# The second parts of the first 16 weight tiles move from GpSimd to VectorE

## The chip, the cores and the metric

The kernel runs on one core of a Trainium2 chip. The metric is the device time of one execution in microseconds (us); the median of several executions is compared. PE is TensorE, DVE is VectorE, ACT is ScalarE, POOL is GpSimd, and SP is the queue that issues every load and store of this kernel.

## The reference

Retention (attention without softmax, with a decaying mask) over 8 batches and 8 heads gives 4608 rows of 512; a feed-forward layer with a rational activation follows, all in float32. The weights arrive as float64.

```python
scores = scale * np.matmul(q, k.transpose(0, 1, 3, 2))       # 8, 8, 576, 576
ret = scores * Dmat[None, :, :, :]                           # gamma ** (i - j), lower triangle
x = np.matmul(ret, v)                                        # then rows of B * S, H * D = 4608, 512
h = x @ w_in                                                 # w_in 512, 2048
h2 = h * h; h3 = h2 * h
P = a[0] + a[1] * h + a[2] * h2 + a[3] * h3
Q = 1.0 + np.abs(b[0]) * np.abs(h) + np.abs(b[1]) * h2
out = (P / (Q + 1e-06)) @ w_out                              # w_out 2048, 512
```

## The kernel before

**Two parts of each operand.** TensorE multiplies in a rounded 32-bit format. To keep precision, x, g (the activation) and the weights are held as a rounded part and the rest, and every product is three matmuls: first times first, first times second, second times first.

**Weights.** There are 32 weight tiles of 128 x 512: `in 0` to `in 15` (w_in, used by `gemm1`) and `out 0` to `out 15` (w_out, used by `gemm2`). Each is loaded as float64 words (`bits`) and made into float32 on the chip by `split_weight`, in four steps with a `yield` between: ACT takes the absolute value of the upper words into `c`; DVE shifts `c` (TENSOR_SCALAR, called **the shift** here); two scalar_tensor_tensor operations on DVE put in the lower bits (`low`) and the sign (`high`, called **the last combine**); then ACT writes the first part `w[:, 0]` (**the copy**) and GpSimd writes the second part `w[:, 1] = c - w[:, 0]` (**the subtraction**). `c` has four buffers, freed by the subtraction. The order in which the tiles are needed is `order`: in 0, in 1, in 2, in 3, out 0, in 4, out 1, in 5, out 2, in 6, out 3, in 7, out 4, out 5, out 6, out 7 are its first 16, and its last 16 follow.

**Units and steps.** There are 36 units of 128 rows of the retention. For each, GpSimd scales q (`scale_q`), ACT scales v, TensorE makes `scores`, DVE multiplies them by the mask (`decay`, tile `s`), TensorE makes `outputs`, ACT and DVE split the result into `xhi` and `xlo`, and DVE and GpSimd update the state `S_sb` (`add`, `fade`). The first units run before the feed-forward part begins (`before`), the others inside its steps. A step (b, f) makes 128 columns of h for 512 rows: `gemm1` on TensorE, then `ffn_p` (ACT and DVE), `ffn_p2` (DVE, called **p2**; it frees the buffer of h, of which there are two), `ffn_v`, and one step later `ffn_r` (ACT: Ln, Exp) and `ffn_q` on DVE, whose first operation is called **q1** here. `ffn_hi` and `ffn_lo` split g; in the first 24 steps `ffn_lo` runs on GpSimd. `gemm2` adds g times w_out three or four steps later.

**What sets the order.** Each of the engines PE, ACT, DVE and POOL runs its instructions in the order in which the Python code calls them (class `InOrder`); only SP's order is left to the scheduler. Within a step the order is that of a list of names: `BEFORE` for the first units, `FIRST` for steps 0 to 23, and others after that. In `FIRST` the last combine (`split2`) is followed, for DVE, by what `split3` gives it (nothing so far), then `add`, `keep_lo` and p2:

```python
FIRST = (
    "split1 gemm1 outputs ffn_p split2 ffn_hi keep_hi ffn_lo gemm2 ffn_r scale_q split3 add fade keep_lo start ffn_p2"
    " scale_v scores decay split0 ffn_q ffn_v"
).split()
```

`STARTS` says how many weight tiles a step takes up. Of the first 16 tiles, in 0 to in 3 are finished before step 0; out 0 and in 4 in step 0; then step 1: out 1; step 2: in 5; step 3: out 2 and in 6; step 4: out 3; step 5: in 7 and out 4; steps 6, 7 and 8: out 5, out 6 and out 7.

Of the kernel before, what the change touches and what calls it, by code (L numbers as in the profile page):

```python
# [12 lines left out]
F32 = mybir.dt.float32  # L13
# [5 lines left out]
ALU = mybir.AluOpType  # L19
# [10 lines left out]
NF = DFF // P  # L30
# [36 lines left out]
def retention_ffn(ctx: ExitStack, tc: tile.TileContext, qkv, w_in, w_out, ab, masks, gq, gv, out):  # L67
# [22 lines left out]
    pe, act, dve, pool = (InOrder(tc, e) for e in (nc.tensor, nc.scalar, nc.vector, nc.gpsimd))  # L90
# [48 lines left out]
    def split_weight(k):  # L139


        nm = f"{k[0]}_{k[1]}"
        words = bits[k].bitcast(I32).rearrange("p (c w) -> p c w", w=2)
        low, high = words[:, :, 0], words[:, :, 1]
        c = cnv.tile([P, DM], I32, tag="c", name=f"c{nm}")
        cf = c.bitcast(F32)


        act.activation(cf, high.bitcast(F32), AF.Abs, scale=math.ldexp(1.0, -112))
        yield  # L150
        dve.tensor_scalar(c, c, 3, 1, ALU.logical_shift_left, ALU.bitwise_or)
        yield
        dve.scalar_tensor_tensor(c, low, 29, c, ALU.logical_shift_right, ALU.bitwise_or)
        yield
        dve.scalar_tensor_tensor(c, high, -0x80000000, c, ALU.bitwise_and, ALU.bitwise_or)
        yield
        w = wts.tile([P, 2, DM], F32R, tag=f"w{nm}", name=f"w{nm}")
        del bits[k]
        act.activation(w[:, 0, :], cf, AF.Copy)
        pool.tensor_tensor(w[:, 1, :], cf, w[:, 0, :].bitcast(F32), ALU.subtract)  # L160
        parts[k] = w


# [228 lines left out]
    order = [(w, f) for _, w, f in sorted(need)]  # L392
# [7 lines left out]
    def split_start(n):  # L400
        for k in [k for _, k in zip(range(n), splits)]:
            going.append([split_weight(k), 0])
            next(going[-1][0])
# [119 lines left out]
```

## Time and profile before

| what | value |
|---|---|
| time, median of 3 runs (lowest to highest) | 989.28 us (988.65 to 990.79) |
| the profiled execution's own time | 987.99 us |
| its span, first to last instruction | 986.2 us |
| busy share PE, DVE, ACT, POOL | 94%, 84%, 72%, 15% |
| mean granted TensorE clock | 0.985 |

The shares are means over stages with different limits: TensorE is busy nearly all the time only from about 250 us on, and all 32 weight tiles are made before that. A timeline row gives start, duration and engine, and in brackets how long the engine had been idle and what ended that.

### The profile page before, as it was taken

The page shows a single profiled execution, that of the slowest core. Times are in us where ns is not written, and L with a number is a line of the kernel's source. Part 1 is how long each engine was busy: PE and PEld are TensorE (multiplying, and loading weights), DVE is VectorE, ACT ScalarE, POOL GpSimd, SP SyncE. Part 2 cuts the span into 40 slices and gives each one's busy share as a digit, 9 for nine tenths or more (in the row PEclk, how much of TensorE's full clock was granted, in tenths as well). Part 3 has the DMA queues.
Part 4 walks back from the last instruction along what each step waited for, and adds up shares of the span by engine and source line. Part 5 has one row for each costly group of instructions (what it writes and reads, how often), then busy time and mean ns, then how long its engine had stood idle before and what let it go on. Part 6 is the DMA issues. An engine that isn't in the chain of part 4 may idle for free.

```text
span 986.2 us, 14758 instructions
## 1 busy us (share of the span) xinstructions
PE 929.7 (94%) x5658; PEld 752.2 (76%) x5658; DVE 829.3 (84%) x1189; ACT 708.0 (72%) x1274; POOL 146.1 (15%) x128
## 2 busy tenths in 40 slices
PE   7769878779999999999999999999999999999998
PEld 6557666567787888788888888888888888888886
DVE  3899989998789888888888887888788888888895
ACT  5577777778676777777777777777777777777775
POOL 3445333442100000000000000100000000000000
PEclk8799999999999999999999999999999999999999
DMA  9945000003212111210021112110211121001001
GB/s 346 407 160 213 1 0 1 1 0 109 91 59 86 44 44 41 71 56 22 32 81 44 44 44 86 44 65 22 86 44 44 43 86 44 1 1 44 1 1 43
DMA packets 20550, 65.31 MB, mean 66 GB/s; under 512 B 2304, under 2 KB 2432, under 8 KB 20480
## 3 DMA queue, kind: packets, MB, share of 16 engines
q1 hardware_dynamic: 20480, 64.37, 17.9%
q8 instruction: 44, 0.72, 0.3%
q14 instruction: 26, 0.21, 0.1%
HBM read 54.93 MB, written 9.44 MB: 65 GB/s over the span
## 4 chain that ended last, share of the span: by engine, by line
PE 71%; DVE 19%; ACT 5%; issue 3%; DMA 1%; SPq 0%; ACTq 0%; DVEq 0%
PE acc L63 32%; PE h L63 31%; PE ps L63 8%; DVE c L63 8%; DVE p L63 7%; DVE v L63 2%; ACT c L63 1%; ACT u L63 1%; DMA kv<-in_qkv 1%; ACT kv L63 1%; ACT v L63 1%; DVE s L63 1%; ACT o L63 1%; DMA qk<-in_qkv 0%; DVE xlo L63 0%
## 5 line engine op out<-in xcount | busy, mean ns | idle before, releaser
L63 PE MATMUL acc<-w,g 128*128 128x512 f32 x1632 | 402.3, 396 | 5.1 <-ACT o L63 4.0
L63 PE MATMUL h<-xhi,w 128*128 128x512 f32 x1152 | 381.9, 393 | 18.5 <-DVE p L63 17.3
L63 PEld LDWEIGHTS acc<-w,g 128*128 128x128 f32 x1632 | 303.3, 189 | 76.4 <-ACT o L63 4.8
L63 PEld LDWEIGHTS h<-xhi,w 128*128 128x128 f32 x1152 | 216.8, 188 | 70.0 <-DVE p L63 22.7
L63 PE MATMUL h<-xlo,w 128*128 128x512 f32 x576 | 225.1, 391 | 0.2 <-DVE xlo L63 0.2
L63 ACT ACTIVATE p<-h,ab_sb 128x512 f32<-128x512 f32 x144 | 111.4, 773 | 138.7 <-PE h L63 131.5
L63 DVE TENSOR_TENSOR p<-p,h 128x512 f32<-128x512 f32 x144 | 98.9, 687 | 44.3 <-ACT u L63 44.0
L63 DVE SCALAR_TENSOR_TENSOR p<-p,ab_sb,u 128x512 f32<-128x512 f32 x144 | 108.9, 756 | 27.0 <-ACT u L63 26.3
L63 ACT ACTIVATE u<-h 128x512 f32<-128x512 f32 x144 | 85.6, 595 | 60.0 <-DVE v L63 58.5
L63 PEld LDWEIGHTS h<-xlo,w 128*128 128x128 f32 x576 | 108.4, 188 | 22.5 <-DVE xlo L63 0.5
L63 DVE TENSOR_TENSOR v<-v,u 128x512 f32<-128x512 f32 x144 | 99.5, 691 | 27.8 <-ACT v L63 27.7
L63 ACT ACTIVATE v<-u,absb 128x512 f32<-128x512 f32 x144 | 116.3, 808 | 1.4 <-DVE p L63 1.1
L63 DVE SCALAR_TENSOR_TENSOR p<-p,ab_sb,h 128x512 f32<-128x512 f32 x144 | 107.1, 744 | 3.1
L63 ACT ACTIVATE u<-u,lnb 128x512 f32<-128x512 f32 x144 | 104.5, 725 | 4.7
L63 POOL TENSOR_TENSOR S_sb<-S_sb,gv_sb 128x256 f32<-128x256 f32 x32 | 20.4, 638 | 575.8 <-DVE S_sb L63 572.6
L63 DVE SCALAR_TENSOR_TENSOR p<-v,p 128x512 f32<-128x512 f32 x144 | 100.6, 699 | 5.0
L63 ACT ACTIVATE u<-v,lnb 128x512 f32<-128x512 f32 x144 | 103.3, 718 | 0.2 <-DVE v L63 0.2
L63 DVE SCALAR_TENSOR_TENSOR v<-v,u 128x512 f32<-128x512 f32 x144 | 99.4, 691 | 0.0
L63 DVE TENSOR_TENSOR g<-p,g 128x512 fp32r<-128x512 f32 x112 | 90.2, 805 | 1.4 <-ACT g L63 1.4
L63 ACT ACTIVATE g<-p 128x512 fp32r<-128x512 f32 x136 | 85.7, 630 | 6.9 <-DVE p L63 3.3
L63 ACT ACTIVATE kv<-kv,gv_sb 128x64 f32<-128x64 f32 x288 | 72.6, 341 | 10.0 <-DMA gv_sb<-in_gv 6.3
L63 DVE SCALAR_TENSOR_TENSOR c<-bits,c 128x512 int32<-128x512 int32 x64 | 57.8, 914 | 0.1
(35 smaller groups left out, 623.7 us busy)
## 6 DMA issues: line engine op xcount, KB each, us to landing
qk<-in_qkv SPq DMA_DIRECT2D x36, 512.0 KB, 4.8
kv<-in_qkv SPq DMA_DIRECT2D x36, 512.0 KB, 3.9
bits<-in_w_in SPq DMA_DIRECT2D x16, 512.0 KB, 10.2
bits<-in_w_out SPq DMA_DIRECT2D x16, 512.0 KB, 10.2
out<-o SPq DMA_DIRECT2D x16, 512.0 KB, 3.2
out<-o SPq DMA_DIRECT2D x4, 256.0 KB, 2.3
gq_sb<-in_gq SPq DMA_DIRECT2D x1, 256.0 KB, 2.7
mask_sb<-in_masks SPq DMA_DIRECT2D x1, 128.0 KB, 6.3
```

What stands on the lines that cost most here:

```text
L63: return lambda *a, **k: self.tc.keep_in_program_order(method(*a, **k))
```

## The change

For the first 16 tiles of `order` the subtraction is issued on DVE; for the last 16 it stays on GpSimd.

```diff
         act.activation(w[:, 0, :], cf, AF.Copy)
-        pool.tensor_tensor(w[:, 1, :], cf, w[:, 0, :].bitcast(F32), ALU.subtract)
+
+        engine = dve if order.index(k) < NF else pool
+        engine.tensor_tensor(w[:, 1, :], cf, w[:, 0, :].bitcast(F32), ALU.subtract)
         parts[k] = w
```

(`NF` is 16.) On GpSimd 16 subtractions disappear and nothing else changes place. On DVE 16 appear. The first piece is DVE in step 3, where two tiles (out 2 and in 6, written w_2 and w_6 with c_2 and c_6) are finished; p_3 is that step's `ffn_p2` and s the decay of a unit.

```order
 L63 SCALAR_TENSOR_TENSOR c_2_600<-bits_2_484,c_2_600 128x512
 L63 SCALAR_TENSOR_TENSOR c_6_602<-bits_6_486,c_6_602 128x512
+L63 TENSOR_TENSOR w_2_666<-c_2_600,w_2_666 128x512
+L63 TENSOR_TENSOR w_6_669<-c_6_602,w_6_669 128x512
 L63 SCALAR_TENSOR_TENSOR p_3_641<-p_3_641,ab_sb,h_3_626 128x512
 L63 TENSOR_TENSOR s_684<-ps_675,mask_sb 128x1024
```

The two subtractions stand directly behind the two last combines and ahead of p2 and the decay. The second piece is DVE in step 6 (out 5) and at the start of step 7's work, in the changed kernel: c_5 is the last combine, c_6 the shift of the next tile, p_5 with u_5 is q1.

```order
L63 SCALAR_TENSOR_TENSOR c_5_840<-bits_5_622,c_5_840 128x512
L63 TENSOR_TENSOR w_5_931<-c_5_840,w_5_931 128x512
L63 TENSOR_TENSOR S_sb<-S_sb,ps_843 128x256
L63 TENSOR_TENSOR xlo_458<-ps_843,xhi_457 128x4x128
L63 SCALAR_TENSOR_TENSOR p_6_908<-p_6_908,ab_sb,h_6_865 128x512
L63 TENSOR_SCALAR c_6_937<-c_6_937 128x512
L63 SCALAR_TENSOR_TENSOR p_5_811<-p_5_811,ab_sb,u_5_809 128x512
```

Only the row of w_5 is new there; the six others stood in this order before. The third piece is SP's queue, where the loads of one later unit (qk_734 and kv_736, unit 8) and of weight tiles stand.

```order
-L102 DMA qk_734<-in_qkv 128x1024
-L104 DMA kv_736<-in_qkv 128x1024
 L137 DMA bits_11_1096<-in_w_out 128x512
 L137 DMA bits_15_1098<-in_w_in 128x512
 L137 DMA bits_12_1150<-in_w_out 128x512
+L104 DMA kv_736<-in_qkv 128x1024
+L102 DMA qk_734<-in_qkv 128x1024
```

The unit's two loads move behind three weight loads; the rest of SP's order is as it was.

## Rows read from the trace of the kernel before

**Rows 1.** Windows: length, busy PE, PEld, DVE, ACT, POOL, then clock, DMA, GB/s.
```profile
300.00:350.00 50.00, 49.43 (x316) 40.14 (x315) 43.35 (x64) 35.78 (x66) 3.75 (x4) 1.00 0.18 64
```
**Rows 2.** Chain that ended last, 50 to 112 us, by line.
```profile
by line: DVE c L63 43.3%; DVE p L63 29.1%; DVE v L63 8.6%; issue 7.1%; DVE s L63 5.5%; DVE xlo L63 2.9%; ACT c L63 2.1%; DVE S_sb L63 1.6%; ACT w L63 0.1%
```
**Rows 3.** Tiles c and g: count, duration in ns (min/median/max), first and last start.
```profile
L63 DVE TENSOR_SCALAR c<-c x32: 412/1070/1520, 18.5 to 220.9; 128x512 int32<-128x512 int32 x32
L63 DVE TENSOR_TENSOR g<-p,g x112: 678/684/1334, 240.8 to 977.9; 128x512 fp32r<-128x512 f32 x112
```
**Rows 4.** Timeline, step 7 (out 6): start, duration, engine, instruction.
```profile
101.36 1.19 DVE L63 SCALAR_TENSOR_TENSOR c<-bits,c 128x512 int32<-128x512 int32 x1
102.48 0.73 DVE L63 SCALAR_TENSOR_TENSOR p<-p,ab_sb,h 128x512 f32<-128x512 f32 x1
103.80 1.07 DVE L63 TENSOR_SCALAR c<-c 128x512 int32<-128x512 int32 x1 [0.59 <-ACT c L63]
104.79 0.74 DVE L63 SCALAR_TENSOR_TENSOR p<-p,ab_sb,u 128x512 f32<-128x512 f32 x1
102.59 0.63 ACT L63 ACTIVATE w<-c 128x512 fp32r<-128x512 f32 x1 [0.82 <-DVE c L63]
103.29 1.30 POOL L63 TENSOR_TENSOR w<-c,w 128x512 fp32r<-128x512 f32 x1 [1.29 <-ACT w L63]
```
**Rows 5.** Timeline, step 1 (out 1): the copy and q1.
```profile
51.88 0.63 ACT L63 ACTIVATE w<-c 128x512 fp32r<-128x512 f32 x1
54.07 0.74 DVE L63 SCALAR_TENSOR_TENSOR p<-p,ab_sb,u 128x512 f32<-128x512 f32 x1
```
**Rows 6.** Timeline, step 2 (in 5): GpSimd's scaling of q, the copy, two shifts.
```profile
58.46 1.75 POOL L63 TENSOR_TENSOR qk<-qk,gq_sb 128x512 f32<-128x512 f32 x1
59.08 0.64 ACT L63 ACTIVATE w<-c 128x512 fp32r<-128x512 f32 x1 [0.42 <-DVE c L63]
60.56 1.94 DVE L63 TENSOR_SCALAR c<-c 128x512 int32<-128x512 int32 x2
```
**Rows 7.** Timeline, step 3 (out 2, in 6): both copies, the decay, q1.
```profile
68.60 1.23 ACT L63 ACTIVATE w<-c 128x512 fp32r<-128x512 f32 x2 [2.00 <-DVE c L63]
69.75 1.21 DVE L63 TENSOR_TENSOR s<-ps,mask_sb 128x1024 f32<-128x1024 f32 x1
72.02 0.74 DVE L63 SCALAR_TENSOR_TENSOR p<-p,ab_sb,u 128x512 f32<-128x512 f32 x1
```
**Rows 8.** Timeline, steps 3 to 5: outputs, ACT's xhi and copy, two shifts, later outputs.
```profile
71.06 1.98 PE L63 MATMUL ps<-s,kv 128*64 128x128 f32 x16 [5.46 <-ACT c L63]
75.02 0.60 ACT L63 ACTIVATE xhi<-ps 128x512 fp32r<-128x512 f32 x1 [0.26 <-PE ps L63]
77.03 0.63 ACT L63 ACTIVATE w<-c 128x512 fp32r<-128x512 f32 x1
78.50 1.94 DVE L63 TENSOR_SCALAR c<-c 128x512 int32<-128x512 int32 x2
89.02 1.09 PE L63 MATMUL ps<-s,kv 128*64 128x128 f32 x16 [1.07 <-ACT c L63]
```
**Rows 9.** Timeline, step 6 (out 5): the copy, the shift, ffn_q's second operation.
```profile
95.01 0.64 ACT L63 ACTIVATE w<-c 128x512 fp32r<-128x512 f32 x1 [0.42 <-DVE c L63]
96.48 0.82 DVE L63 TENSOR_SCALAR c<-c 128x512 int32<-128x512 int32 x1
98.24 0.68 DVE L63 SCALAR_TENSOR_TENSOR v<-v,u 128x512 f32<-128x512 f32 x1
```
**Rows 10.** Timeline, before step 0: DVE and GpSimd around in 0, TensorE after it.
```profile
23.55 1.51 DVE L63 TENSOR_SCALAR c<-c 128x512 int32<-128x512 int32 x1
25.10 1.63 DVE L63 SCALAR_TENSOR_TENSOR c<-bits,c 128x512 int32<-128x512 int32 x1
24.74 1.45 POOL L63 TENSOR_TENSOR qk<-qk,gq_sb 128x512 f32<-128x512 f32 x1
30.41 2.08 PE L63 MATMUL ps<-qk 64*128 64x128 f32 x16 [6.72 <-DVE xlo L63]
```

## The prediction

> **What bounds the kernel now.** I read the windows first, to see which engine is full in which stage. From 300 to 350 us TensorE is busy 49.43 of 50 us [rows 1]; there a GpSimd or DVE instruction more or less would not show. But the last of the 32 weight tiles is shifted at 220.9 [rows 3], so I asked for the chain of work that ended last in the stretch with the first 16, after the first units: from 50 to 112 us it lies on DVE with about 91% (c 43.3, p 29.1, v 8.6, s 5.5, xlo 2.9, S_sb 1.6), and with 2.2% on ACT [rows 2]. TensorE does not stand in that list at all. So whatever makes DVE's sequence longer there makes the kernel longer, and the shift lasts: behind it come the same DVE chain for the last 16 tiles and then the full TensorE.
>
> **What a tile costs DVE now.** Then I read the timeline of one step, step 7, where out 6 is finished [rows 4]. The last combine starts at 101.36 and takes 1.19. Its record ends at 102.55, and p2 starts at 102.48: a record outlasts the start of the next operation by 0.07, which I take off everywhere. ACT's copy starts at 102.59 and takes 0.63. GpSimd subtracts from 103.29 to 104.59. DVE is done with p2 and waits 0.59 for ACT (which takes the absolute value of the next tile after the copy); its shift then takes 1.07, where the shortest shift of the run takes 0.41 [rows 3]. It ends 0.28 after GpSimd's subtraction, so it stood still while GpSimd read SBUF. Then q1 starts at 104.79.
>
> The Trainium skill (SBUF — State Buffer, § Who interferes with whom) says that GpSimd and DVE share a pair of ports and that the second to come is blocked until the first is done, for a DVE operation with two SBUF inputs or in a two-port mode. The shift's end behind GpSimd's agrees.
>
> **The change part by part.** *The new operation.* The trace has no weight subtraction on DVE, but it has the same form: DVE's `g<-p,g`, 128x512 from two SBUF inputs, median 0.684 [rows 3], so 0.61 until the next operation can start. *The removed one* costs no time on GpSimd, which idles; what goes is its hold on DVE. *The new wait.* In the changed order the subtraction stands right behind the last combine on DVE, but needs ACT's copy, which needs that last combine. So DVE, which runs in order, waits: copy 0.63 and 0.03 to start. Before, it did p2 and the decay meanwhile. Queued behind it are p2 (for which TensorE's next `gemm1` waits), the decay (for which `outputs` waits), the next shift and ffn_q. The stretch from copy to q1 can therefore be worked out step by step. p2 is 0.66, the decay 1.14 (1.21 less 0.07 [rows 7]), a free shift 0.34.
>
> Step 7: now 104.79 - 102.59 = 2.20. Changed: 0.66 + 0.61 + 0.66 + 0.34 = 2.27; the wait for ACT's absolute value lies under the subtraction, and the stretch of the shift is gone. **+0.07.** Step 8 is built alike, +0.07. Two tiles cost next to nothing, though each gets a wait.
>
> Step 1: now 54.07 - 51.88 = 2.19 [rows 5]. Changed, with the decay: 0.66 + 0.61 + 0.66 + 1.14 + 0.34 = 3.41. **+1.22**: here the decay covered almost all of GpSimd's subtraction, and little stretch is won back.
>
> Step 2: GpSimd's scaling of q runs from 58.46 to 60.21 [rows 6], where now nobody on DVE needs the port. The subtraction, ready at 59.08 + 0.67 = 59.75, must wait until 60.21, and 0.47 later the next can start (so it is for the combine at 25.10, held until 26.19 and followed at 26.66 [rows 10]): 60.68. Now what stands there starts at 58.97 (copy's start less 0.11). That is +1.71; the two shifts fall from 1.94 (1.87 without the overlap) to 0.68, which is -1.19. **+0.52.**
>
> Step 3, two tiles: the copies run from 68.60 to 69.83 [rows 7]; the first subtraction fits under the second copy. 69.83 + 0.03 + 0.61 = 70.47 for p2, 71.13 for the decay, 72.27 for the shift, 72.61 for q1, now 72.02. **+0.59**, and step 5 alike, +0.59.
>
> Step 4: the decay of step 3 starts at 71.13 and not at 69.75, 1.38 late, while q1 is only 0.59 late. `outputs` waits for it: the 16 matmuls at 71.06 came after 5.46 of idle time, and ACT's xhi at 75.02 waited for them with hardly any slack (0.26) [rows 8]. ACT is in order, so the copy at 77.03 moves to 78.41. Then the next operation on DVE after the subtraction starts at 78.41 + 0.66 + 0.61 = 79.68 in place of 76.92: +2.76, less 1.19 for two shifts (again 1.94) = +1.57, of which 0.59 came from step 3. **+0.98.** At step 5 the matmuls of `outputs` idle only 1.07 now and xhi has slack, so I don't carry it on.
>
> Step 6: 95.01 + 0.64 + 0.03 + 0.61 = 96.29 in place of 94.90, +1.39 [rows 9]; the shift and q1 fall from 1.76 (96.48 to 98.24) to 0.34 + 0.66. **+0.63.**
>
> Sum of steps 1 to 8: 0.07 + 0.07 + 1.22 + 0.52 + 0.59 + 0.59 + 0.98 + 0.63 = **+4.7**.
>
> *Before step 1.* Around in 0 the chain runs through DVE: its shift takes 1.51 and its first combine 1.63, both held by GpSimd, 3.11 together (23.55 to 26.66), and TensorE waits 6.72 for what DVE does after them [rows 10]. Changed: 0.61 + 0.45 + 0.60 = 1.66, and the scaling of q (24.74) may still hold DVE for all of a 1.30 (a lone GpSimd operation of that size, rows 4's) or not at all. So a gain between 0.15 and 1.45; I take the middle, **-0.8**. For in 1 the chain goes through TensorE next. For in 2, in 3, out 0 and in 4 I cost nothing: DVE then waits for the first h and for ACT's v, and GpSimd's hold on the shifts goes away; with that cover gone it would be 4 x 0.61 = 2.4.
>
> *SP.* The loads of unit 8 move behind three weight loads; that unit is scaled in step 22, many steps after. Nothing.
>
> Total: 4.7 - 0.8 = **+3.9**. On the profiled execution's 987.99 that is 991.9; that execution lies 1.29 under the median of 989.28, so the median should be **993.2**. Bounds: step 4's lag absent (0.98 becomes 0.52) and the full gain at in 0 give +2.8; the smallest gain and the cover gone give 4.7 - 0.15 + 2.4 = +7.0.
>
> **The rivals.** *Faster: the port was the whole cost.* If each of the 16 subtractions held DVE for all its 1.30, 20.8 us would go, against 16 x 0.61 = 9.8 for the new ones and some 8 waits of 0.67, 5.4: -5.6, or 983.7. It decides as soon as DVE loses more than 0.95 per removed subtraction. Against it: step 7's shift lost 0.66, step 1's is hardly stretched [rows 4, 5]; what DVE reads from PSUM runs on. Chance 0.10.
>
> The Trainium skill (GPSIMD Engine Reference, § 4.1 Engine selection) sends elementwise work of two inputs to VectorE, with GpSimd about twice as slow. Duration against duration the trace agrees (1.30 to 0.68), and by that alone the sum would be 16 x 0.62 = 9.9 less, 979.4; but no GpSimd instruction stands in the chain.
>
> *No change: the delay is taken up.* DVE's waits for ACT (0.59 in step 7) and the change-over to TensorE could swallow what the steps lose: 989.3. For it: that wait disappears, which I counted. Against it: each later wait on ACT is for something that ACT does after DVE's own last combine, so it moves along. Chance 0.17.
>
> *Slower still: TensorE's clock.* After 5.46 idle the 16 matmuls took 1.98, after 1.07 idle 1.09 [rows 8]. In step 5 the decay comes late too, by 1.38 and the lag of step 4, and the idle time grows to nearly 3. If the clock falls there, the 48 matmuls of `outputs` cost 0.9 to 2 more, and step 6 gets step 4's lag: about 994.7. Chance 0.18.
>
> My forecast as worked out: 0.55. About 0.2% (2 us) is what a measurement of this kernel can tell from no change. Chances: slower 0.73, within 0.2% 0.17, faster 0.10. The range for 8 in 10 runs from 990.2 to 995.8: the sum's bounds less their far corner, the clock rival and the upper part of no change; the likeliest case alone spans 992 to 994.5.
>
> **What would show it.** Right: DVE's 16 subtractions of about 0.68, those of steps 1, 4, 6, 7 and 8 with 0.6 to 0.7 of idle time in front put down to ACT's copy; shifts back at 0.4 in steps 1 to 8; q1 of step 7 at the same distance from its copy; the later stages shifted by a constant. Wrong: copies that are done when DVE comes (faster), GpSimd's scaling or `ffn_lo` holding the new subtractions everywhere (slower), or the first h of the feed-forward part coming over 1 us later or earlier than worked out.

## The result and the profile after

The changed kernel takes 992.13 us (median of 11 runs, 989.21 to 994.56), the kernel before 988.54 in the same comparison (11 runs, 986.04 to 990.79). The ratio is 1.0037, 95% interval 1.0025 to 1.0049, so the change costs 3.6 us, between 2.5 and 4.8. The forecast was 993.2, 3.9 more than the median of 989.28 that was then known; against 988.54 the same sum gives 992.4.

The profiled execution has a span of 990.0 us, 3.8 more than that of before. The page's first lines show what each engine did in it:

```profile
span 990.0 us, 14742 instructions
...
PE 930.8 (94%) x5658; PEld 753.4 (76%) x5658; DVE 827.8 (84%) x1205; ACT 707.7 (71%) x1274; POOL 124.8 (13%) x112
```

DVE has 16 instructions more and yet is busy 1.5 us less (829.3 in the profile before): the new subtractions take 11.3, but the shifts fall from 34.6 to 24.4 and the combines from 57.8 to 55.4. If busy time set the end, this kernel would not be slower. The view of tile w shows the new operation, and who waited:

```profile
L63 DVE TENSOR_TENSOR w<-c,w x16: 678/693/1207, 23.1 to 113.0; 128x512 fp32r<-128x512 f32 x16
L63 POOL TENSOR_TENSOR w<-c,w x16: 1276/1294/1305, 120.4 to 233.9; 128x512 fp32r<-128x512 f32 x16
...
  DVE w L63: 5.2, 7
```

The last line is from the list of who waited: DVE stood idle 5.2 us, seven times, ahead of a subtraction (0.16 in step 0, the rest in steps 1, 2, 4, 6, 7 and 8; in steps 3 and 5, with two tiles each, it didn't wait). The same wait in a single step, the timeline of step 7, against [rows 4]:

```profile
103.86 1.19 DVE L63 SCALAR_TENSOR_TENSOR c<-bits,c 128x512 int32<-128x512 int32 x1
105.09 0.63 ACT L63 ACTIVATE w<-c 128x512 fp32r<-128x512 f32 x1 [0.83 <-DVE c L63]
105.75 0.69 DVE L63 TENSOR_TENSOR w<-c,w 128x512 fp32r<-128x512 f32 x1 [0.69 <-ACT w L63]
106.36 0.74 DVE L63 SCALAR_TENSOR_TENSOR p<-p,ab_sb,h 128x512 f32<-128x512 f32 x1
107.02 0.42 DVE L63 TENSOR_SCALAR c<-c 128x512 int32<-128x512 int32 x1
107.35 0.74 DVE L63 SCALAR_TENSOR_TENSOR p<-p,ab_sb,u 128x512 f32<-128x512 f32 x1
```

The last combine ends, ACT copies, and for 0.69 DVE does nothing; p2, which followed the last combine at once before, starts only at 106.36. The shift is back at 0.42. From the copy to q1 it is 2.26, against 2.20 before and 2.27 in the forecast.

Step 1, against [rows 5], where the decay stands behind p2:

```profile
49.99 0.63 ACT L63 ACTIVATE w<-c 128x512 fp32r<-128x512 f32 x1
50.65 0.69 DVE L63 TENSOR_TENSOR w<-c,w 128x512 fp32r<-128x512 f32 x1 [0.70 <-ACT w L63]
51.26 0.74 DVE L63 SCALAR_TENSOR_TENSOR p<-p,ab_sb,h 128x512 f32<-128x512 f32 x1
51.92 1.22 DVE L63 TENSOR_TENSOR s<-ps,mask_sb 128x1024 f32<-128x1024 f32 x1
53.05 0.42 DVE L63 TENSOR_SCALAR c<-c 128x512 int32<-128x512 int32 x1
53.38 0.75 DVE L63 SCALAR_TENSOR_TENSOR p<-p,ab_sb,u 128x512 f32<-128x512 f32 x1
```

From the copy to q1 it is 3.39, forecast 3.41, before 2.19. The wait is as long as in step 7, but here the shift had little to give back.

Steps 3 and 4, against [rows 7, 8]:

```profile
69.11 1.30 DVE L63 TENSOR_TENSOR w<-c,w 128x512 fp32r<-128x512 f32 x2
70.99 1.22 DVE L63 TENSOR_TENSOR s<-ps,mask_sb 128x1024 f32<-128x1024 f32 x1
72.31 1.98 PE L63 MATMUL ps<-s,kv 128*64 128x128 f32 x16 [5.92 <-ACT p L63]
76.27 0.60 ACT L63 ACTIVATE xhi<-ps 128x512 fp32r<-128x512 f32 x1 [1.07 <-PE ps L63]
78.14 0.62 ACT L63 ACTIVATE w<-c 128x512 fp32r<-128x512 f32 x1
78.79 0.69 DVE L63 TENSOR_TENSOR w<-c,w 128x512 fp32r<-128x512 f32 x1 [1.37 <-ACT w L63]
80.98 0.75 DVE L63 TENSOR_SCALAR c<-c 128x512 int32<-128x512 int32 x2
```

This is the chain that the forecast drew over four engines: the decay late, TensorE's `outputs` late, ACT's xhi waiting for it (1.07, before 0.26), the copy behind xhi late, and DVE idle for 1.37 in front of the subtraction.

The chain of work that ended last from 50 to 112 us, by line, to set beside [rows 2]:

```profile
by line: DVE c L63 17.6%; DVE p L63 14.7%; PE ps L63 11.9%; DMA bits<-in_w_out 10.7%; PE h L63 7.4%; issue 7.4%; ACT w L63 6.0%; DVE w L63 4.4%; DVE v L63 3.1%; ACT v L63 2.3%; ACT p L63 2.2%; ACT u L63 2.2%; DVE xlo L63 1.9%; ACT c L63 1.9
```

The copy and the subtraction now stand in it with 6.0% and 4.4%, before with 0.1% and nothing. The view follows TensorE and a load for part of the way, so the shares of c and p are not to be set against those of before; for the loss I go by positions.

To follow the loss through the steps I compared the start of q1 in both profiles. ACT's first operation on the first h stands for the start, at 42.23 before and 40.33 after. In step 6 the second operation of ffn_q is compared, as in the forecast (before, q1 itself took 1.10 there in place of 0.74).

| place | before | after | after - before | added in the step | forecast |
|---|---|---|---|---|---|
| first h | 42.23 | 40.33 | -1.90 | | |
| step 1 | 54.07 | 53.38 | -0.69 | +1.21 | +1.22 |
| step 2 | 62.42 | 62.25 | -0.17 | +0.52 | +0.52 |
| step 3 | 72.02 | 72.45 | +0.43 | +0.60 | +0.59 |
| step 4 | 80.36 | 81.66 | +1.30 | +0.87 | +0.98 |
| step 5 | 89.99 | 91.86 | +1.87 | +0.57 | +0.59 |
| step 6 (ffn_q's second operation) | 98.24 | 100.73 | +2.49 | +0.62 | +0.63 |
| step 7 | 104.79 | 107.35 | +2.56 | +0.07 | +0.07 |
| step 8 | 112.07 | 114.64 | +2.57 | +0.01 | +0.07 |

Steps 1 to 8 lose 4.47, forecast 4.7. Then the distance stays at +2.6 until step 23, as "the later stages shifted by a constant" asks, and is +3.4 at step 26 (242.07 and 245.50). Two things are left: the 1.90 by which the changed kernel is ahead at the first h, where the forecast had 0.8, and the 0.8 near step 24, where it had nothing.

The rows put most of both down to TensorE's clock. Windows around the first `gemm1`, in the first fence before and in the second after; the third number from the end of a row is the granted clock:

```profile
37.80:42.20 4.40, 4.38 (x13) 3.04 (x15) 4.40 (x3) 0.37 (x2) 3.95 (x3) 0.61 1.03 412
37.50:40.30 2.80, 2.58 (x9) 1.97 (x9) 2.80 (x3) 0.67 (x3) 2.67 (x3) 0.70 1.03 411
```
```profile
37.50:40.30 2.80, 2.80 (x13) 2.07 (x15) 2.80 (x5) 0.35 (x2) 0.52 (x1) 1.00 1.01 405
```

In the stretch from 37.50 to 40.30 the kernel before has a clock of 0.70 and 9 matmuls, the changed one 1.00 and 13. ACT's first operation on h comes 4.42 after TensorE's first xlo matmul before (37.81 to 42.23) and 2.83 after (37.50 to 40.33): 1.6 of the 1.90 is the clock of this one `gemm1`. And the timeline has `outputs` of unit 8, before and after:

```profile
221.11 1.09 PE L63 MATMUL ps<-s,kv 128*64 128x128 f32 x16 [3.35 <-ACT c L63]
```
```profile
223.74 1.98 PE L63 MATMUL ps<-s,kv 128*64 128x128 f32 x16 [3.36 <-ACT c L63]
```

The same 16 matmuls after the same idle time take 0.9 longer (granted clock 1.00 from 221.10 to 222.20 before, 0.50 from 223.74 to 225.72 after); the distance of 0.8 appears within the three steps behind them. Whether the change does that, or chance, was a question for the experiments. That this profile's span is longer by 3.8, so near the forecast of 3.9, is in part luck: -1.6 and +0.8 of clock stand in it.

From 300 to 350 us TensorE is as full as in [rows 1]:

```profile
300.00:350.00 50.00, 49.43 (x316) 39.97 (x315) 43.60 (x63) 34.87 (x65) 3.75 (x4) 1.00 0.19 64
```

### The profile page after: what moved, and what is told of

The parts are those of the page before. It is cut to its first block, busy times and chain, and to the rows that moved or that the text cites. A ratio compares the mean times of both kernels' runs of the same rounds, so it can differ in the third digit from the quotient of the medians.

```text
span 990.0 us, 14742 instructions
## 1 busy us (share of the span) xinstructions
PE 930.8 (94%) x5658; PEld 753.4 (76%) x5658; DVE 827.8 (84%) x1205; ACT 707.7 (71%) x1274; POOL 124.8 (13%) x112
## 4 chain that ended last, share of the span: by engine, by line
PE 74%; DVE 13%; DMA 5%; ACT 5%; issue 2%; SPq 0%; ACTq 0%; DVEq 0%
PE acc L63 33%; PE h L63 31%; PE ps L63 9%; DVE c L63 5%; DVE p L63 5%; DMA bits<-in_w_in 3%; DMA bits<-in_w_out 2%; DVE v L63 2%; ACT u L63 1%; ACT c L63 1%; DMA qk<-in_qkv 1%; ACT v L63 1%; ACT o L63 1%; ACT kv L63 1%; ACT w L63 1%
## 5 line engine op out<-in xcount | busy, mean ns | idle before, releaser
L63 PE MATMUL ps<-s,kv 128*64 128x128 f32 x576 | 43.3, 297 | 18.5 <-ACT p L63 11.8
```

Of the source, the lines that this page charges most:

```text
L63: return lambda *a, **k: self.tc.keep_in_program_order(method(*a, **k))
```

## The experiments

The theory: the cost is DVE's wait for ACT's copy, since the subtraction stands directly behind the last combine; the operation itself is about paid for by the shifts. The rivals: DVE has 16 operations more in a stretch in which it is full, and that costs wherever they stand; or the loss comes from one place (before step 1, or TensorE's clock).

**The subtraction behind p2 and the decay.** A further `yield` and a further stage put the same 16 subtractions of DVE ahead of the shift instead of behind the last combine.

```diff
-BEFORE = "... keep_hi keep_lo split3 split0".split()
+BEFORE = "... keep_hi keep_lo split3 split4 split0".split()
...
-    " scale_v scores decay split0 ffn_q ffn_v"
+    " scale_v scores decay split4 split0 ffn_q ffn_v"
...
+        on_dve = order.index(k) < NF
+        if on_dve:
+            yield
```

> The 16 subtractions stay on VectorE, but stand after p2 and the decay of the step, ahead of the next shift, so that ACT's copy is done when VectorE comes to them. Theory (the wait for the copy is what the change costs; the operation itself is paid by the shift that is no longer stretched): no idle time in front of the subtractions of steps 1 to 8; against the kernel before, q1 moves by +0.45 in step 1, -0.3 in 2, +0.4 in 3, -0.5 in 4, +0.4 in 5, -0.1 in 6 and -0.6 in 7 and 8 each, -0.8 in sum, and with the gain before step 1 the time is 1 to 2.5 us under the kernel before. Rival (the operation: VectorE is full, so 10 more operations cost about 6 us wherever they stand): as the changed kernel, 3 to 4 us over the kernel before.

Measured: 985.79 (12 runs) against 988.22 of before, ratio 0.997 [0.9959, 0.9981]: 2.4 faster than before, where the changed kernel is 3.6 slower. Step 7 in its timeline:

```profile
98.83 1.19 DVE L63 SCALAR_TENSOR_TENSOR c<-bits,c 128x512 int32<-128x512 int32 x1
99.94 0.73 DVE L63 SCALAR_TENSOR_TENSOR p<-p,ab_sb,h 128x512 f32<-128x512 f32 x1
100.05 0.63 ACT L63 ACTIVATE w<-c 128x512 fp32r<-128x512 f32 x1 [0.82 <-DVE c L63]
100.71 0.69 DVE L63 TENSOR_TENSOR w<-c,w 128x512 fp32r<-128x512 f32 x1
101.32 0.42 DVE L63 TENSOR_SCALAR c<-c 128x512 int32<-128x512 int32 x1
101.65 0.75 DVE L63 SCALAR_TENSOR_TENSOR p<-p,ab_sb,u 128x512 f32<-128x512 f32 x1
```

The subtraction has the same 0.69, and no bracket: p2 lies over the copy. From the copy to q1 it is 1.60, against 2.26 in the changed kernel and 2.20 before. So the 16 operations, with what the freed shifts give back, cost nothing on balance, and the rival of the full DVE falls. That the time came out as expected is in part luck: by the profile the steps gain 2.4 and not 0.8. Steps 3 and 5 came out at -0.2 each in place of +0.4, since GpSimd's `ffn_lo` falls on other combines there and holds them less (in step 3 the four take 3.05, before 3.64); behind step 23 about 1.0 is lost again.

**The same place, without the wait.** The first 16 subtractions stay directly behind the last combine, but subtract a constant that lies ready in place of ACT's copy. These second parts aren't those of the weights; all else is computed as before.

```diff
-        engine = dve if order.index(k) < NF else pool
-        engine.tensor_tensor(w[:, 1, :], cf, w[:, 0, :].bitcast(F32), ALU.subtract)
+        if order.index(k) < NF:
+            dve.tensor_tensor(w[:, 1, :], cf, gq_sb.rearrange("p g i -> p (g i)"), ALU.subtract)
+        else:
+            pool.tensor_tensor(w[:, 1, :], cf, w[:, 0, :].bitcast(F32), ALU.subtract)
```

> The changed kernel, with the 16 subtractions at the same place on VectorE, but taking a constant tile from c in place of the first part, so that they need no copy from ACT (the second parts of these 16 tiles are thereby not the reference's). Theory of the wait: no idle time in front of them in steps 1, 4, 6, 7 and 8; against the kernel before +0.45, +0.5, +0.4, +0.5, +0.4, -0.15, -0.65 and -0.65 in steps 1 to 8, +0.8 in sum, and with the gain before step 1 the time is within 1.5 us of the kernel before and 3 to 4.5 under the changed one. Rival (the operation, not the wait): as the changed kernel, 3 to 4 us over the kernel before.

Measured: 989.82 (12 runs), ratio 1.0012 [1.0001, 1.0023]: 1.6 above before (0.1 to 2.3), 2.0 less than what the changed kernel loses. The direction is as expected, both amounts miss their bounds, narrowly on the first and by 1 us on the second. Steps 2 and 4 cost 0.5 each, as expected: the subtraction, which no longer waits, comes 0.9 and 1.3 earlier in GpSimd's scaling of q and is held by it. Step 4:

```profile
77.98 1.75 POOL L63 TENSOR_TENSOR qk<-qk,gq_sb 128x512 f32<-128x512 f32 x1
78.60 1.68 DVE L63 TENSOR_TENSOR w<-c,gq_sb 128x512 fp32r<-128x512 f32 x1
```

1.68 in place of 0.69, until 0.5 after GpSimd's end. So in those two steps the wait for ACT had hidden a wait for the port. The Trainium skill (SBUF — State Buffer, § Who interferes with whom) says that of a DVE operation with two SBUF inputs and a GpSimd operation that reads SBUF the second waits for the whole of the first; these rows agree.

The miss is in step 7, which gains 0.1 and not 0.65. There the last combine, which takes 1.19 in the profiles of before and of the changed kernel, takes 1.66 while GpSimd's `ffn_lo` runs from 103.63 to 104.92:

```profile
103.81 1.66 DVE L63 SCALAR_TENSOR_TENSOR c<-bits,c 128x512 int32<-128x512 int32 x1
```

In the profile steps 1 to 8 lose 1.57 without the wait (0.8 expected) and 4.46 with it. So by the profiles the wait accounts for 2.9 of the loss, by the times for 2.0 of 3.6; the rest is what the operations cost where the shifts have little to give back, and the port. Behind step 23 this profile loses 1.0 more; unit 8's 16 matmuls took 1.93 in it.

**Only the tiles of steps 1 to 8, and only those ahead of step 1.**

```diff
-        engine = dve if order.index(k) < NF else pool
+        engine = dve if 6 <= order.index(k) < NF else pool
```

> Of the first 16 tiles only the last 10 (steps 1 to 8) are subtracted on VectorE, in the place of the changed kernel; the first 6 stay on GpSimd. Theory (the sum of steps 1 to 8): from the v of step 0 to q1 of step 8 the profile is 4.7 longer than before (4.5 in the changed kernel's profile), and the time is 3 to 6 us over the kernel before. Rival (TensorE's clock and the first units make the difference of the two kernels, not these steps): less than 2 us over the kernel before.

Measured: 992.42 (6 runs) against 988.28, ratio 1.0048 [1.003, 1.0066]: 4.1 slower, as expected, and the rival falls. From the v of step 0 to q1 of step 8 its profile is 4.43 longer than before, expected 4.7. The other part:

```diff
-        engine = dve if order.index(k) < NF else pool
+        engine = dve if order.index(k) < 6 else pool
```

> Only the first 6 tiles (before step 1) are subtracted on VectorE; the other 26 stay on GpSimd. Theory (gain of 0.8 at in 0, between 0.15 and 1.45, the other five hidden): the time is 0 to 2 us under the kernel before. Rival (their cover is gone): 4 x 0.61 = 2.4 for in 2, in 3, out 0 and in 4, so 1 to 2.5 us over the kernel before.

Measured: 988.13 (12 runs), ratio 0.9993 [0.9981, 1.0005]: -0.15, between -1.9 and +0.5, no change that can be measured. The expected gain of 0 to 2 isn't contradicted, the rival (1 to 2.5 over) is. The loss is all in steps 1 to 8; the two parts add to +4.0, the whole change measured +3.6.

The position of q1 against the profile before, at steps 1 and 8, sets the kernels side by side; the difference of the two is what happens in between, and leaves out how each execution began.

| kernel | step 1 | step 8 | between them |
|---|---|---|---|
| changed | -0.69 | +2.57 | +3.26 |
| steps 1 to 8 alone | +0.72 | +3.95 | +3.23 |
| changed, without the wait | +0.63 | +1.66 | +1.03 |
| ahead of step 1 alone | -3.52 | -4.18 | -0.66 |
| behind p2 and the decay | -0.99 | -3.79 | -2.80 |

In steps 1 to 8 the kernel that is changed ahead of step 1 alone has the code of before, so its -0.66 shows how far a single profile can be off. Of it 0.58 arises in step 5, where `ffn_lo` falls on other combines as in the first experiment; it does so too in the kernel of the next experiment, whose steps 1 to 6 are also unchanged.

What each step costs against before, step 1 counted from the v of step 0:

| step | changed | steps 1 to 8 alone | without the wait: expected | measured | behind p2 and the decay: expected | measured |
|---|---|---|---|---|---|---|
| 1 | +1.20 | +1.20 | +0.45 | +0.54 | +0.45 | +0.42 |
| 2 | +0.52 | +0.85 | +0.5 | +0.51 | -0.3 | -0.49 |
| 3 | +0.60 | +0.60 | +0.4 | +0.43 | +0.4 | -0.19 |
| 4 | +0.87 | +0.53 | +0.5 | +0.52 | -0.5 | -0.50 |
| 5 | +0.57 | +0.56 | +0.4 | +0.39 | +0.4 | -0.21 |
| 6 | +0.62 | +0.61 | -0.15 | -0.05 | -0.1 | -0.16 |
| 7 | +0.07 | +0.08 | -0.65 | -0.12 | -0.6 | -0.60 |
| 8 | +0.01 | 0.00 | -0.65 | -0.65 | -0.6 | -0.65 |
| sum | +4.46 | +4.43 | +0.8 | +1.57 | -0.8 | -2.38 |

**The last 18 tiles, directly behind the last combine.** Steps 7 and 8 cost next to nothing with the wait. If that is so, the later steps that are built alike cost as little.

```diff
-        engine = dve if order.index(k) < NF else pool
+        engine = dve if order.index(k) >= NF - 2 else pool
```

> The subtractions of out 6, out 7 and the last 16 tiles on VectorE right behind the last combine, as in the changed kernel; the first 14 stay on GpSimd. Theory (each step worked out from its own rows): steps 7 to 20 cost +0.07 each, 1.0 in all, steps 21 to 24 between 0 and +1.5 together; the time is 1 to 2.5 us over the kernel before, although 18 waits of 0.67 appear. Rival (every tile costs its wait): 18 x 0.67 = 12 us of waits show in full, or at least 0.3 per tile, 5 us and more.

Measured: 993.08 (6 runs) against 988.22, ratio 1.0043 [1.0027, 1.0059]: 4.9 slower (2.7 to 5.8), more than expected and near the rival's 5. By steps the expectation holds for 13 of them: from step 8 to step 21 the distance to before grows from -2.25 to -1.30, 0.07 each. By step 25 it is +2.07, 3.3 more than at step 22, and there the expectation (0 to 1.5) failed. Step 23, where the decay stands behind the subtraction as in step 1, costs 1.5 of it; step 24 costs another 2.8, of which step 25 gives 1.0 back. The timeline of step 24, where out 15 is finished:

```profile
229.02 2.01 ACT L63 ACTIVATE kv<-kv,gv_sb 128x64 f32<-128x64 f32 x8
230.93 0.62 ACT L63 ACTIVATE w<-c 128x512 fp32r<-128x512 f32 x1
231.58 0.69 DVE L63 TENSOR_TENSOR w<-c,w 128x512 fp32r<-128x512 f32 x1 [2.56 <-ACT w L63]
```

Here ACT scales a unit's v, eight operations in 2.01, before it comes to the copy, and DVE waits 2.56. So the length of the wait depends on what ACT has in front of the copy. The rival's price of 0.3 or more for every tile is not what the 13 steps show.

**All 32 tiles behind p2**, with the stage in the later steps' lists too:

```diff
-    " ffn_p2 scores decay split3 ffn_q"
+    " ffn_p2 scores decay split3 split4 ffn_q"
...
+        on_dve = order.index(k) < 2 * NF
+        if on_dve:
+            yield
```

> As the first, but all 32 subtractions on VectorE, after p2 and the decay. Theory of the wait: in each of steps 7 to 20 the stretch from copy to q1 falls by 0.6 (from 2.20 to 1.61), so 12 more steps give -7 and steps 21 to 24 about -1; the time is 8 to 11 us under the kernel before. Rival (the operation): 32 x 0.61 less the stretch of the shifts, or at least 3 us over the kernel before.

Measured: 978.65 (6 runs), ratio 0.9901 [0.9885, 0.9917]: 9.6 faster than before, as expected. From step 8 to step 21 each step is 0.6 shorter (7.22 before, 6.62 here), and at step 22 q1 lies 12.9 ahead; about 4 of it is lost again by step 28, where the expectation had a further gain of 1 for steps 21 to 24. Part of that loss is out 15, with the same wait as above:

```profile
218.85 0.69 DVE L63 TENSOR_TENSOR w<-c,w 128x512 fp32r<-128x512 f32 x1 [2.55 <-ACT w L63]
```

**The same with out 15 left on GpSimd** (`2 * NF - 1` in place of `2 * NF`):

> As the run with all 32 late on VectorE, but the last tile (out 15) stays on GpSimd: there VectorE idled 2.55 for ACT's copy, which stands behind the 8 scalings of v on ACT. Theory (idle time in front of the subtraction is the cost): 2 to 2.5 us under that run, so 10 to 14 us under the kernel before. Rival (the idle time there is taken up by the wait for TensorE that follows): the same time as that run within 1 us.

Measured: 978.24 (4 runs) against 988.28, ratio 0.99 [0.9882, 0.9919], 0.4 below the version with all 32 and not to be told from it: the rival's forecast, not the theory's 2 to 2.5. In its profile 2.55 is won at step 24 (q1 12.25 ahead of before, not 9.70), but by step 28 only 1.1 of it is left (9.73, not 8.63). There DVE waits for others:

```profile
226.65 0.42 DVE L63 COPY S_sb<-ps 128x256 f32<-128x256 f32 x1 [1.28 <-ACT xhi L63]
...
239.18 1.23 DVE L63 TENSOR_TENSOR s<-ps,mask_sb 128x1024 f32<-128x1024 f32 x1 [0.85 <-PE ps L63]
```

In this stretch DVE waits for ACT and TensorE, so time that it wins ahead of it is worth only what they can take up. How the 3 lost between step 22 and step 28 divide between TensorE's clock and its load I didn't separate.

**The kernel before, once more**, as a look at how far the same code moves:

> The kernel before once more, for a second profile. Theory (part of the 1.9 us by which the changed kernel's profile is ahead at step 0 is TensorE's clock in the first matmuls of gemm1, which differs between executions): the start of ffn_p in step 0 and q1 of later steps move by up to 2 us against the first profile with the same code. Rival (it is the change): they agree within 0.3 us.

Measured: 989.67, one run, span 987.7 against 986.2. From step 1 to step 23 every q1 that I compared lies 1.1 earlier than in the first profile of the same code; from there to step 28 it loses 2.6 and stays 1.5 behind. A window of this second profile:

```profile
245.00:255.00 10.00, 10.00 (x83) 7.84 (x85) 5.82 (x8) 4.36 (x8) 0.00 (x0) 0.83 0.27 103
```

The clock is 0.83 from 245 to 255, where the first profile has 1.00; TensorE is busy for all 10 us in both. So differences of 1 to 3 us at the first h and near step 24 occur with no change in the code. The 0.8 of the changed kernel's profile doesn't go with the change either. Where only steps 1 to 8 are changed, unit 8's 16 matmuls took 1.09, and the distance stays at +3.96 from step 8 to step 28. Where only the tiles ahead of step 1 are, they took 1.98 after 3.33 of idle time, and 0.9 is lost there.

## Why the prediction was right

**Steps 1 to 8** hold one by one in the changed kernel's profile, and as a sum in a second one. The sum was 4.7; the profile shows 4.47, that of the kernel that changes only these tiles 4.43, and the latter's time is 4.1 longer. The wait ahead of the subtraction is there as announced in steps 1, 6, 7 and 8 (0.69 to 0.70) and is twice that in step 4 (1.37). Taking it away by another place takes away all of the loss, by another operand 2.0 of the 3.6. Two steps need a remark:

- *Step 2* has the forecast sum and not its parts, which is luck. The forecast let the subtraction be ready 0.46 before GpSimd's scaling ended and be held until then.

```profile
56.73 0.60 ACT L63 ACTIVATE xhi<-ps 128x512 fp32r<-128x512 f32 x1 [0.61 <-PE ps L63]
57.77 1.75 POOL L63 TENSOR_TENSOR qk<-qk,gq_sb 128x512 f32<-128x512 f32 x1
58.60 0.62 ACT L63 ACTIVATE w<-c 128x512 fp32r<-128x512 f32 x1
59.25 0.82 DVE L63 TENSOR_TENSOR w<-c,w 128x512 fp32r<-128x512 f32 x1 [0.88 <-ACT w L63]
59.99 0.41 DVE L63 TENSOR_TENSOR S_sb<-S_sb,ps 128x256 f32<-128x256 f32 x1
```

The copy came 0.2 later against the rest of the step than before, because ACT's xhi had waited 0.61 for TensorE, whose 16 matmuls of step 1 took 1.97 where they took 1.09 before. So DVE waited longer for ACT (0.88) and hardly for the port (the subtraction took 0.82 instead of 0.68). The next operation starts 1.02 after that of before; with the lead of 0.69 that the step began with this is the +1.71 worked out.

- *Step 4* cost 0.87 and not 0.98: the copy, held up by xhi, was late by 1.28 (78.14 - 77.03, and 0.17 of lead), not 1.38.

Both depend on when TensorE is done with `outputs`. In the profile of the kernel that changes steps 1 to 8 alone ACT's xhi waited 1.07 for it in step 2 and 0.64 in step 4, and the two steps cost 0.85 and 0.53. The close agreement of these two is that of one execution.

**Before step 1** the -0.8 was the middle between two bounds, and mis-sized. Between the two xlo around in 0 the changed kernel needs 6.16 (22.53 to 28.69), before 6.51: a gain of 0.35. It is no accident of one execution: the three other profiles in which this code is unchanged have 6.51 or 6.52, and that of the kernel changed only ahead of step 1 has 6.15. DVE's timeline there, against [rows 10]:

```profile
23.14 0.68 DVE L63 TENSOR_TENSOR w<-c,w 128x512 fp32r<-128x512 f32 x1
23.54 1.40 POOL L63 TENSOR_TENSOR qk<-qk,gq_sb 128x512 f32<-128x512 f32 x1 [0.98 <-DMA qk<-in_qkv]
23.74 1.49 DVE L63 TENSOR_SCALAR c<-c 128x512 int32<-128x512 int32 x1
25.26 0.69 DVE L63 SCALAR_TENSOR_TENSOR c<-bits,c 128x512 int32<-128x512 int32 x1
```

GpSimd, relieved of its subtraction, starts the scaling of q at 23.54 instead of 24.74 (0.8 earlier, with the 0.4 taken off by which this execution is ahead there), and now that holds the shift for 1.49; only the combine is free (0.69, before 1.63). The scaling holds DVE for 1.1 (1.49 for a shift of 0.41), close to the 1.30 of the lower bound. The first h came 1.90 earlier, 1.1 more than the 0.8 worked out, and the prediction had named more than 1 us there as a sign that it is wrong. But the rest of the 1.90 isn't the change: an execution of the kernel before, and kernels whose code is unchanged up to there, show it too: ACT's first operation on h, at 42.23 in the first profile of before, is at 41.11 in its second, at 40.84 where only the tiles of steps 1 to 8 are moved, and at 39.58 where only the last 18 are. That in 2, in 3, out 0 and in 4 cost nothing agrees with the rows of step 0: from ACT's first operation on h to the next `v` on DVE it is 7.12 before (42.23 to 49.35) and 7.13 after (40.33 to 47.46). Two profiles with that code unchanged have 8.0 there, so what decides it is the time of the kernel changed only ahead of step 1, 0.15 under before.

With 0.35 for 0.8 the terms give 4.47 - 0.35 = 4.1, within the measured 2.5 to 4.8.

**The rivals.** *The port was the whole cost* fell: the shifts did come back to 0.42, but nowhere more than worked out. *The delay is taken up* fell: the distance stays the same from step 8 to step 23. *GpSimd's slower subtraction* (979.4, duration against duration) fell with the time. *TensorE's clock* did not fall where I put it: the matmuls of step 5 idled 2.91, near the 3 expected, and kept the full speed (granted clock 1.00):

```profile
91.71 1.09 PE L63 MATMUL ps<-s,kv 128*64 128x128 f32 x16 [2.91 <-ACT p L63]
```

It fell in step 1, as said under step 2, and at unit 8. Since the same code moves at unit 8 by as much, and the kernel that changes steps 1 to 8 alone loses nothing there, I don't count that 0.8 as the change's.

## What to carry to other kernels

On an engine that runs in order, an operation costs its duration and also the wait that its place brings: the same 16 operations of 0.69 us cost 3.6 us directly behind the operation whose result ACT first has to copy for them, and won 2.4 us one or two operations later. The Trainium skill (GPSIMD Engine Reference, § 4.1 Engine selection) sends elementwise work of two inputs from GpSimd to VectorE; here that pays (9.6 us with all 32 late) once ACT, the engine in between, does its part while DVE has other work. To price such a move, work out the stretch from the input to the next operation that others wait for, with the shared port and with what the producing engine has queued ahead, step by step: seven of eight steps came out within 0.06 us of such a working in one profile, six of eight within 0.08 in another, the sums within 0.3.

## What was not expected of the hardware

TensorE's granted clock differs between executions at the same place after the same idle time. The 16 matmuls of unit 8's `outputs` took 1.09 after 3.35 of idle time in one profile and 1.98 after 3.36 in another; in the changed kernel the 16 matmuls of step 5 took 1.09 after 2.91, those of step 1 took 1.97 after 2.97:

```profile
53.24 1.97 PE L63 MATMUL ps<-s,kv 128*64 128x128 f32 x16 [2.97 <-ACT p L63]
```

The granted clock over the long ones is 0.50 (223.74 to 225.72, 53.24 to 55.20), which is 1.2 GHz, and over the short ones 1.00 (221.10 to 222.20, 91.71 to 92.80), which is 2.4 GHz. So an idle time alone, near 3 us, doesn't say in this kernel which of the two the next matmuls get. One profile of each kernel would have put the 1.6 us of the first h down to the change; a second profile of the unchanged code, and medians of 4 to 23 runs, were needed to leave them out.
